# Gradient of two cached-attention blocks on one core: staging tiles, buffer counts, load order and the K transposes are rearranged

## The chip, the core and the metric

The kernel runs on one core of a Trainium2 chip. The time is the device time of one launch in microseconds (us). Of the kernel before there are 11 runs; a comparison of this kernel cannot tell less than about 0.5% from no change.

## What is computed

The forward function has two equal blocks, A and B, with their own inputs; each computes

```
q = x @ wq                         # x [8, 96, 640], wq [640, 32*128]
p = softmax(q k^T / sqrt(128))     # k_cache, v_cache [8, 32, 512, 128]
o = p v
a = o @ wo                         # wo [32*128, 640]
```

and the two results are joined on the last axis. The kernel returns this output and, for a given grad_out [8, 96, 1280], the gradients of all ten inputs (x, k_cache, v_cache, wq and wo of both blocks). Everything is bfloat16. With 8 batch rows b, 32 heads h and two blocks there are 512 pairs (h, b), each with 96 queries and 512 keys.

## The kernel before

One core does block A and then block B. Within a block the heads follow each other, and within a head the eight batch rows. A pair (h, b) passes through stages that are spread over successive **ticks**, one pair entering per tick: transposing K on TensorE (PE) where that is done (`c_s1`, L260), the scores S and their row maximum (`c_s2a`, L271), the exponential E (L284), the normalised P (L304, on GpSimd, POOL), P transposed and the output O from V (`c_s45`, L313), dV (`c_s4`, L341), dP, a row sum and dS (`c_s6`, L371), dS transposed and dQ from K (`c_s78`, L385), dK (`c_s7`, L411). So in each tick PE works on several pairs at once, in different stages.

Per head there is more: wo and wq are loaded (`pA`, L172, from POOL's queue), transposed (`pB`), Q and dO are projected (`pC`, L207: `q_ps`) and transposed (`pD`), O and dQ are transposed back (`qA`), dwo and dwq are made (`qB`, L445; `qD`, L465). Heads are put together in groups of five or six; at the end of a group `gU` (L487) adds the group's part of the output and of dx. With the block's last group the sums go to tiles `ob` and out by DMA.

The order of all this is written by hand: an emitter sorts all steps by a tick and a slot (tables OFF, HK and SLOTS, L45 to L51). A scheduler then takes them in that order, and moves above all DMAs to where their buffers come free; `pinned` (L107) keeps an instruction in program order among those that are pinned.

K and V come from memory in pairs of batch rows, 256 KB a load, from SyncE's queue (SP), into rings of 7 K and 5 V buffers. Of both a transposed copy is needed: V's (`VT`, 3 buffers) is always made by a DMA transpose (`c_xt`, L252, on SP's queue); K's (`KT`, 2 buffers) is made so for the odd pairs of a head, and on PE for the even ones: four 128x128 transposes (L265) per b and a copy out of PSUM on VectorE (DVE, L267). So half of K is transposed on PE.

At the start (`first`), x and grad_out are loaded whole (`setup_nat`, L134) and transposed (`setup_T`, L118). For block B they are needed while block A still runs and still uses its own copies. So they come a second time, in twelve tiles of [128, 640] (160 KB) from POOL's queue (`setup_ld`, L110), into a pool of their own of 6 buffers (`ld_tmp`), and PE transposes them during the last heads of block A. After A is done, the whole arrays follow (L146).

Of the kernel before, what the change touches and what calls it, by code (L numbers as in the profile page):

```python
# [10 lines left out]
F32 = mybir.dt.float32  # L11
# [29 lines left out]
SL_HEAD = 90  # L41
SL_GRP = 95
SL_SETUP = 96

OFF = dict(ldk=-5, ldv=-3, kt=-1, vt=2, s2=3, s3=3, s4=4, s5=5, s6=6, s7=7, s8=8)  # L45
HK = dict(pA=-7, pB=-3, pC0=[-2, 0], pC1=[-1, 0], pD1=1, pD0=2, qA0=13, qA1=17, qB=[20, 17], qD=[(18, 0, 2), (19, 2, 4), (20, 4, 5)])
EV = dict(pB0="act", pB1="dve", pC00="act", pC01="act", pC10="act", pC11="dve", pD0="dve", pD1="dve", qA0="dve", qA1="dve", qB0="act", qB1="act", qD="dve", gU="act")
GSPREAD0 = 9
PRIO_OFF = 2000
# [4 lines left out]
def build_block(tc, em, tick0, blk, x, kc, vc, wq, wo, g_all, out_all, dx, dk, dv, dwq, dwo, ident, ones, pools, HG=6, first=True, groups=None):  # L54
# [47 lines left out]
    HS = pools["HS"]  # L102
    CS = pools["CS"]

    stp = pools["stp"]

    def pinned(ins):  # L107
        return tc.keep_in_program_order(ins)

    def setup_ld(which_, t):  # L110
        def f():
            src_flat = x_flat if which_ == 0 else g_flat
            tmp = stp.tile([128, D], BF16, name="ld_tmp")
            pinned(nc.gpsimd.dma_start(tmp[:], src_flat[t * 128:(t + 1) * 128, :]))
            S[("tmp", which_, t)] = tmp
        return f

# [47 lines left out]
    for i, (which_, t) in enumerate(xg):  # L165
        if not first:
            em.add(tick0 - 12 + i // 2, SL_LOAD, setup_ld(which_, t))
        em.add(tick0 + ((-8 if which_ == 0 else -3) if first else -8 + i // 2), SL_SETUP, setup_T(which_, t))
    em.add(tick0 + (-11 if first else B + OFF["s5"] - 2), SL_LOAD + 1, setup_nat(1))
    em.add(tick0 + (-12 if first else B + OFF["s8"] - 2), SL_LOAD, setup_nat(0))  # L170

    def pA(h):  # L172
        def f():
            wo_h = hst.tile([128, D], BF16, name="wo_h", bufs=HG + 3)
            order = pinned if first and 0 < h < HG + 3 else (lambda ins: ins)
            if h % 2 == 0:
                wq_p = hd.tile([128, DC, 256], BF16, name="wq_p", bufs=2)
                with nc.allow_non_contiguous_dma(reason="wq slice of two heads"):
                    order((nc.sync if first and h == 0 else nc.gpsimd).dma_start(wq_p[:], wq_v[:, :, h * 128:(h + 2) * 128]))
            order(nc.gpsimd.dma_start(wo_h[:], wo[h * 128:(h + 1) * 128, :]))  # L180
            if h % 2 == 1:
                wq_p = HS[(blk, h - 1)]["wq_p"]
            HS[(blk, h)] = dict(wo_h=wo_h, wq_p=wq_p, wq_h=wq_p[:, :, (h % 2) * 128:(h % 2 + 1) * 128])
        return f
# [261 lines left out]
    def qB(h, di):  # L446
        def f():
            st = HS[(blk, h)]
            Onat = st["Onat"]
            if "dwo_sb" not in st:  # L450
                st["dwo_sb"] = hd.tile([128, D], BF16, name="dwo_sb", bufs=1)
                st["dwo_n"] = 0
            dwo_sb = st["dwo_sb"]
            (c0, w) = dsplits[di]
            w_ps = bank([128, w], F32, "dwo_ps")
            for t in range(TT):
                nc.tensor.matmul(w_ps[:], Onat[:, t, :], S["g_nat"][:, t, c0:c0 + w], start=(t == 0), stop=(t == TT - 1))  # L457
# [30 lines left out]
    def gU(g, which, t, gi):  # L488
        def f():
            acc = S.get("out_acc" if which == 0 else "dx_acc")  # L490
            dst_flat = out_flat if which == 0 else dx_flat
            (c0, w) = gsplits[gi]
            o_ps = bank([128, w], F32, "o_ps")
            for hh in range(groups[g]):
                h = GH0[g] + hh
                src = HS[(blk, h)]["OT_h"] if which == 0 else HS[(blk, h)]["dQT_h"]
                rhs = HS[(blk, h)]["wo_h"][:, c0:c0 + w] if which == 0 else HS[(blk, h)]["wqT_h"][:, c0:c0 + w]
                nc.tensor.matmul(o_ps[:], src[:, t * 128:(t + 1) * 128], rhs, start=(hh == 0), stop=(hh == groups[g] - 1))  # L498
            if 0 < g < NG - 1:
                nc.vector.tensor_tensor(acc[:, t, c0:c0 + w], o_ps[:], acc[:, t, c0:c0 + w], op=ALU.add)  # L500
                return
            if g == 0 and NG > 1:
                evac(EV["gU"], acc[:, t, c0:c0 + w], o_ps[:])
                return
            if gi == 0:
                S["ob"] = wk.tile([128, D], BF16, name="ob", bufs=4)
            ob = S["ob"]
            if NG == 1:
                evac(EV["gU"], ob[:, c0:c0 + w], o_ps[:])
            else:  # L510
                nc.vector.tensor_tensor(ob[:, c0:c0 + w], o_ps[:], acc[:, t, c0:c0 + w], op=ALU.add)
            if gi == len(gsplits) - 1:
                (nc.gpsimd if first else nc.sync).dma_start(dst_flat[t * 128:(t + 1) * 128, :], ob[:])
        return f

    NTS = len(tsplits)
    S45 = pools["S45"]
    S78 = pools["S78"]
    for g in range(NG):
        h0 = GH0[g]  # L520
        for hh in range(groups[g]):
            h = h0 + hh
            c0t = tick0 + h * B
            if not (first and h == 0):
                em.add(c0t + HK["pA"], SL_LOAD, pA(h))
            em.add(c0t + HK["pB"], SL_HEAD, pB(h))
            for si in range(NTS):
                em.add(c0t + HK["pC0"][min(si, len(HK["pC0"]) - 1)], SL_HEAD, pC(h, 0, si))
                em.add(c0t + HK["pC1"][min(si, len(HK["pC1"]) - 1)], SL_HEAD, pC(h, 1, si))
            em.add(c0t + HK["pD1"], SL_HEAD, pD(h, 1))  # L530
            em.add(c0t + HK["pD0"], SL_HEAD, pD(h, 0))
            for b in range(B):
                ct = c0t + b
                if b % NB == 0:
                    em.add(tick0 - 12 if first and h == 0 and b == 0 else ct + OFF["ldk"], SLOTS["LOAD"], c_ld(h, b, "K", 7))
                    em.add(ct + OFF["ldv"], SLOTS["LOAD"], c_ld(h, b, "V", 5))
                    if (b // NB) % 2 == 1:
                        em.add(ct + OFF["kt"], SLOTS["LOAD"] + 1, c_xt(h, b, "KT", 2))
                    em.add(ct + OFF["vt"], SLOTS["LOAD"] + 1, c_xt(h, b, "VT", 3))
                if (b // NB) % 2 == 0:  # L540
                    em.add(ct + 2, SLOTS["S1"], c_s1(h, b))
                em.add(ct + OFF["s2"], SLOTS["S2A"], c_s2a(h, b))
                em.add(ct + OFF["s2"], SLOTS["S2B"], c_s2b(h, b))
                em.add(ct + OFF["s3"], SLOTS["S3A"], c_s3a(h, b))
                em.add(ct + OFF["s3"], SLOTS["S3B"], c_s3b(h, b))
                em.add(ct + OFF["s5"], SLOTS["S5B"], c_s5b(h, b))
                if b % 2 == 1:
                    em.add(ct + OFF["s4"] + 1, SLOTS["LOAD"], c_st(h, b, "v"))
# [35 lines left out]
def _kernel_impl(tc, A_x, A_k_cache, A_v_cache, A_wq, A_wo, B_x, B_k_cache, B_v_cache, B_wq, B_wo, grad_out,  # L584
# [13 lines left out]
    with ExitStack() as ctx:  # L598
# [3 lines left out]
        make_identity(nc, ident[:])  # L602
        ones = cst.tile([128, 1], BF16, name="ones")
        nc.vector.memset(ones[:], 1.0)
        pools = dict(
            const=P(name="const", bufs=1),
            ps=P(name="ps", bufs=8, space=PSUM),
# [2 lines left out]
            hd=P(name="hd", bufs=2),  # L610
            hst=P(name="hst", bufs=HG + 2),
            grp=P(name="grp", bufs=1),
            stp=P(name="stp", bufs=6),
        )
        pools["S45"] = {}
        pools["S78"] = {}
        pools["HS"] = {}
# [80 lines left out]
```

## Time and profile before

| what | value |
|---|---|
| median of 11 runs | 1745.0 us (1735.7 to 1760.11) |
| the profiled execution: its time | 1745.14 us |
| its span, first to last instruction | 1743.1 us |
| mean granted clock of TensorE | 0.994 |
| busy: ACT, DVE, POOL | 81%, 77%, 60% |
| DMA | 424.69 MB, mean 244 GB/s |
| HBM read, written | 161.09 MB, 159.12 MB |

The span is 2.0 us shorter than the time of the same execution. A busy PE is not PE at its peak: the profile models the end of a matmul, and matmuls are pipelined. What one costs is read from the distance between starts, in the list of instructions in order of time ("timeline"). The busy share of the DMA engines counts every packet in flight, of all queues, over 16 engines; as packets of several queues overlap, it can be over 1. PEclk is the share of its full clock that TensorE was granted.

### The profile page before, as it was taken

The numbers are of one execution on the slowest core, as the hardware profiler recorded it, in microseconds if no ns is written. First come the engines' busy times: TensorE is split into PE (matmuls) and PEld (weight loads), VectorE is DVE, ScalarE is ACT, GpSimd is POOL, SyncE is SP. The second block draws the span as 40 slices with busy tenths as digits, with TensorE's granted clock in tenths as the row PEclk, the third lists the DMA queues.
The fourth block names the chain that finished last, engine by engine and source line by source line (L and its number), as shares of the span: only waits on it lengthen the run. The fifth ranks groups of instructions, "written<-read, shape, count | busy, mean of one in ns | idle before, by whom it ended". The sixth has DMA issues, their size and how long they took to land.

```text
span 1743.1 us, 57509 instructions
## 1 busy us (share of the span) xinstructions
PE 1678.8 (96%) x21730; PEld 1328.2 (76%) x21944; DVE 1334.1 (77%) x3043; ACT 1414.6 (81%) x4023; POOL 1049.1 (60%) x1759
## 2 busy tenths in 40 slices
PE   7999999999999999999898999999999999999998
PEld 6787777778778778777677777787787787787785
DVE  5887677778878878877676876787788787788785
ACT  6998788878879879878667997897798797798793
POOL 3676566556556656557465665565565665565563
PEclk9999999999999999999999999999999999999999
DMA  9999999999989989999999999999999899999893
GB/s 252 266 287 244 244 246 233 266 221 249 247 229 264 262 218 261 260 223 232 228 273 251 271 264 215 240 273 239 218 261 244 222 276 241 219 277 245 205 256 123
DMA packets 603751, 424.69 MB, mean 244 GB/s; under 512 B 425633, under 2 KB 560417, under 8 KB 603473
## 3 DMA queue, kind: packets, MB, share of 16 engines
q1 hardware_dynamic: 548752, 239.22, 69.2%
q0 software_dynamic: 54720, 181.78, 32.8%
q8 instruction: 172, 2.82, 0.7%
q14 instruction: 107, 0.87, 0.2%
HBM read 161.09 MB, written 159.12 MB: 184 GB/s over the span
## 4 chain that ended last, share of the span: by engine, by line
PE 74%; DVE 9%; ACT 7%; DMA 5%; issue 3%; POOL 1%; SPq 0%; ACTq 0%; DVEq 0%; POOLq 0%
PE o_ps L498 11%; PE q_ps L223 11%; PE dwo_ps L457 5%; PE dwq_ps L477 5%; PE S_ps L278 5%; PE dV_ps L349 5%; PE dK_ps L419 5%; PE dP_ps L377 5%; PE dq_dst_ps L402 4%; PE optp_ps L332 4%; PE optp_ps L325 4%; PE dq_dst_ps L395 3%; DVE negm L280 3%; DVE dS_sb L381 3%; ACT E_sb L290 2%
## 5 line engine op out<-in xcount | busy, mean ns | idle before, releaser
L309 POOL TENSOR_SCALAR P_sb<-E_sb,rinv 96x512 bf16<-96x512 bf16 x512 | 350.8, 685 | 403.2 <-DVE rinv L300 399.8
L290 ACT ACTIVATE E_sb<-S_ps,negm 96x512 bf16<-96x512 f32 x512 | 349.2, 682 | 191.4 <-DVE negm L280 186.3
L381 DVE SCALAR_TENSOR_TENSOR dS_sb<-dP_ps,dl_ps,P_sb 96x512 bf16<-96x512 f32 x512 | 383.0, 748 | 97.5 <-PE dl_ps L379 72.1
L280 DVE TENSOR_REDUCE negm<-S_ps 96x1 f32<-96x512 f32 x512 | 347.5, 679 | 64.1 <-PE S_ps L278 59.4
L422 ACT ACTIVATE dK_sb<-dK_ps 128x512 bf16<-128x512 f32 x512 | 301.3, 589 | 59.4 <-PE dK_ps L419 38.1
L352 ACT ACTIVATE dV_sb<-dV_ps 128x512 bf16<-128x512 f32 x512 | 313.5, 612 | 8.7 <-DMA out_dram<-dV_sb 8.6
L358 POOL DMA_DIRECT2D out_dram<-dV_sb x256 | 194.8, 761 | 130.0 <-ACT dV_sb L352 90.9
L338 ACT ACTIVATE PT_sb<-optp_ps 128x384 bf16<-128x384 bf16 x512 | 254.6, 497 | 1.6 <-PE optp_ps L332 1.6
L358 POOL DMA_DIRECT2D out_dram<-dK_sb x256 | 192.3, 751 | 38.2 <-ACT dK_sb L422 28.5
L367 POOL TENSOR_TENSOR prod<-OT_h,dOT_h 128x96 bf16<-128x96 bf16 x512 | 186.1, 363 | 43.4 <-ACT OT_h L335 35.7
L377 PE MATMUL dP_ps<-VT,dOT_h 128*96 128x512 bf16 x512 | 195.8, 382 | 6.0 <-DMA VT<-V_sb 5.6
L349 PE MATMUL dV_ps<-dOnat_h,P_sb 96*128 96x128 bf16 x2048 | 199.1, 220 | 0.0
L419 PE MATMUL dK_ps<-Qnat_h,dS_sb 96*128 96x128 bf16 x2048 | 197.9, 219 | 0.0
L404 DVE COPY dST_sb<-dq_dst_ps 128x384 bf16<-128x384 bf16 x512 | 176.3, 344 | 22.6 <-PE dq_dst_ps L402 22.6
L402 PE MATMUL dq_dst_ps<-ident,dS_sb 96*128 96x96 bf16 x2048 | 172.3, 206 | 11.8 <-DVE dS_sb L381 11.7
L332 PE MATMUL optp_ps<-ident,P_sb 96*128 96x96 bf16 x2048 | 172.4, 206 | 8.7 <-POOL P_sb L309 8.2
L325 PE MATMUL optp_ps<-PT_sb,V_sb 128*128 128x96 bf16 x2048 | 172.5, 206 | 3.0 <-ACT dV_sb L352 3.0
L395 PE MATMUL dq_dst_ps<-dST_sb,K_sb 128*128 128x96 bf16 x2048 | 170.7, 206 | 0.0
L395 PEld LDWEIGHTS <-K_sb 128*128 128x128 bf16 x2048 | 131.8, 98 | 29.4 <-issue 5.2
L300 DVE RECIPROCAL rinv<-rowsum 96x1 f32<-96x1 f32 x512 | 80.3, 157 | 88.2 <-ACT E_sb L290 78.3
L223 PE MATMUL q_ps<-gT,woT_h 128*128 128x512 bf16 (+1 forms) x625 | 137.0, 325 | 0.9
L457 PE MATMUL dwo_ps<-g_nat,Onat 128*128 128x128 bf16 (+1 forms) x708 | 129.6, 294 | 3.6 <-ACT dK_sb L422 0.2
(84 smaller groups left out, 3789.8 us busy)
## 6 DMA issues: line engine op xcount, KB each, us to landing
out_dram<-dV_sb POOLq DMA_DIRECT2D x256, 256.0 KB, 4.7
out_dram<-dK_sb POOLq DMA_DIRECT2D x256, 256.0 KB, 4.8
K_sb<-in_A_k_cache_dram SPq DMA_DIRECT2D x128, 256.0 KB, 4.7
V_sb<-in_A_v_cache_dram SPq DMA_DIRECT2D x128, 256.0 KB, 4.8
K_sb<-in_B_k_cache_dram SPq DMA_DIRECT2D x128, 256.0 KB, 4.5
V_sb<-in_B_v_cache_dram SPq DMA_DIRECT2D x128, 256.0 KB, 4.6
out_dram<-dwo_sb POOLq DMA_DIRECT2D x64, 160.0 KB, 4.5
out_dram<-dwq_sb POOLq DMA_DIRECT2D x32, 320.0 KB, 4.7
```

Source lines behind the costliest of these rows:

```text
L223: nc.tensor.matmul(q_ps[:], lhs(c), rhsT[:, c, t0:t0 + w], start=(c == 0), stop=(c == DC - 1))
L280: nc.vector.tensor_reduce(negm[:], S_ps[:], axis=AX.X, op=ALU.max, negate=True)
L290: nc.scalar.activation(E_sb[:], st["S_ps"][:], ACT.Exp, bias=st["negm"][:], scale=1.0, accum_out=rowsum[:])
L309: nc.gpsimd.tensor_scalar(P_sb[:], st["E_sb"][:], st["rinv"][:], 0.0, op0=ALU.mult, op1=ALU.add)
L349: nc.tensor.matmul(dV_ps[:, c * 128:(c + 1) * 128], P_sb[:, c * 128:(c + 1) * 128], hs["dOnat_h"][:, b * 128:(b + 1) * 128], start=True, s ...
L352: nc.scalar.activation(SB[(blk, h, b // 2, "v")][:, b % 2], dV_ps[:], ACT.Identity, scale=1.0)
L358: nc.gpsimd.dma_start(dst[b - 1:b + 1, h].rearrange("b (p c) d -> p b (c d)", c=KC), SB.pop((blk, h, b // 2, which))[:])
L377: nc.tensor.matmul(dP_ps[:], hs["dOT_h"][:, tok], st["VT"], start=True, stop=True)
L381: nc.vector.scalar_tensor_tensor(dS_sb[:], dP_ps[:], dl_ps[:, 0:1], st["P_sb"][:], op0=ALU.subtract, op1=ALU.mult)
L395: nc.tensor.matmul(dQT_ps, st["K_sb"][:, c, :], st["dST_sb"][:, c * Sq:(c + 1) * Sq], start=(c == 0), stop=(c == KC - 1))
L419: nc.tensor.matmul(dK_ps[:, c * 128:(c + 1) * 128], dS_sb[:, c * 128:(c + 1) * 128], hs["Qnat_h"][:, b * 128:(b + 1) * 128], start=True, s ...
L422: nc.scalar.activation(SB[(blk, h, b // 2, "k")][:, b % 2], dK_ps[:], ACT.Identity, scale=1.0)
```

## The change

- **Staging.** The pool `ld_tmp` goes. The tiles of x for block B are now taken out of the ring of K buffers, those of grad_out out of the ring of V buffers.
- **Buffers.** K 7 to 9, V 5 to 6, KT 2 to 3, VT 3 to 4; the loads and DMA transposes are placed earlier (OFF: ldk -5 to -9, ldv -3 to -5, kt -1 to -2, vt 2 to 0).
- **K on PE.** `k_on_pe`: the first pair of every head, and the third only in heads of even number. So 3 of 8 pairs are transposed on PE, not 4 of 8; the others go by DMA.
- **Output rows.** The tiles `ob` (4 buffers of their own) become buffers of `dwo_sb`, which has 3 instead of 1.
- **Loads of wo and wq.** All but those of the very first head are pinned in program order (before, those of heads 1 to 8 of block A alone); `pA` is placed a tick later.
- **The start.** The transposes of grad_out, the projection of dO and its transposes are put behind the first projection of Q, so that the first S stands ahead of them.
- **PE warmed.** 32 matmuls of a tile of ones, with a result that nobody reads, are the first that PE does.

```diff
-OFF = dict(ldk=-5, ldv=-3, kt=-1, vt=2, s2=3, ...
-HK = dict(pA=-7, ...
+NK_SB, NV_SB = 9, 6
+OFF = dict(ldk=-9, ldv=-5, kt=-2, vt=0, s2=3, ...
+HK = dict(pA=-6, ...
...
-            tmp = stp.tile([128, D], BF16, name="ld_tmp")
-            pinned(nc.gpsimd.dma_start(tmp[:], src_flat[t * 128:(t + 1) * 128, :]))
+            nm, nb_ = ("K_sb", NK_SB) if which_ == 0 else ("V_sb", NV_SB)
+            tmp = kvp.tile([128, NB, KC, 128], BF16, name=nm, bufs=nb_)[:].rearrange("p a c d -> p (a c d)")[:, 0:D]
+            pinned(nc.gpsimd.dma_start(tmp, src_flat[t * 128:(t + 1) * 128, :]))
...
-        em.add(tick0 + ((-8 if which_ == 0 else -3) if first else -8 + i // 2), SL_SETUP, setup_T(which_, t))
+        em.add(tick0 + ((-8 if which_ == 0 else 3) if first else -8 + i // 2), SL_SETUP, setup_T(which_, t))
...
-            order = pinned if first and 0 < h < HG + 3 else (lambda ins: ins)
+            order = (lambda ins: ins) if first and h == 0 else pinned
...
-                st["dwo_sb"] = hd.tile([128, D], BF16, name="dwo_sb", bufs=1)
+                st["dwo_sb"] = hd.tile([128, D], BF16, name="dwo_sb", bufs=3)
...
-                S["ob"] = wk.tile([128, D], BF16, name="ob", bufs=4)
+                S["ob"] = hd.tile([128, D], BF16, name="dwo_sb", bufs=3)
...
+    def k_on_pe(h, b):
+        return b // NB == 0 or (b // NB == 2 and h % 2 == 0)
...
+            fh = first and h == 0
...
-                em.add(c0t + HK["pC1"][min(si, len(HK["pC1"]) - 1)], SL_HEAD, pC(h, 1, si))
-            em.add(c0t + HK["pD1"], SL_HEAD, pD(h, 1))
-            em.add(c0t + HK["pD0"], SL_HEAD, pD(h, 0))
+                em.add(c0t + (3 if fh else HK["pC1"][min(si, len(HK["pC1"]) - 1)]), SL_HEAD + (7 if fh else 0), pC(h, 1, si))
+            em.add(c0t + (3 if fh else HK["pD1"]), SL_HEAD + (8 if fh else 0), pD(h, 1))
+            em.add(c0t + (4 if fh else HK["pD0"]), SL_HEAD, pD(h, 0))
...
-                    if (b // NB) % 2 == 1:
-                        em.add(ct + OFF["kt"], SLOTS["LOAD"] + 1, c_xt(h, b, "KT", 2))
-                    em.add(ct + OFF["vt"], SLOTS["LOAD"] + 1, c_xt(h, b, "VT", 3))
-                if (b // NB) % 2 == 0:
+                    if not k_on_pe(h, b):
+                        em.add(ct + OFF["kt"], SLOTS["LOAD"] + 1, c_xt(h, b, "KT", 3))
+                    em.add(ct + OFF["vt"], SLOTS["LOAD"] + 1, c_xt(h, b, "VT", 4))
+                if k_on_pe(h, b):
                     em.add(ct + 2, SLOTS["S1"], c_s1(h, b))
...
+        warm = cst.tile([128, 128], BF16, name="warm")
+        nc.vector.memset(warm[:], 1.0)
...
-            stp=P(name="stp", bufs=6),
...
+        warm_ps = pools["ps"].tile([128, 128], F32, name="warm_ps", tag="bank")
+        for _ in range(32):
+            nc.tensor.matmul(warm_ps[:], warm[:], warm[:], start=True, stop=True)
```

More of the change, by code (lines that the diff above doesn't have):

```diff
@@ L43 @@
 SL_SETUP = 96
-OFF = dict(ldk=-5, ldv=-3, kt=-1, vt=2, s2=3, s3=3, s4=4, s5=5, s6=6, s7=7, s8=8)
-HK = dict(pA=-7, pB=-3, pC0=[-2, 0], pC1=[-1, 0], pD1=1, pD0=2, qA0=13, qA1=17, qB=[20, 17], qD=[(18, 0, 2), (19, 2, 4), (20, 4, 5)])
+NK_SB, NV_SB = 9, 6
+OFF = dict(ldk=-9, ldv=-5, kt=-2, vt=0, s2=3, s3=3, s4=4, s5=5, s6=6, s7=7, s8=8)
+HK = dict(pA=-6, pB=-3, pC0=[-2, 0], pC1=[-1, 0], pD1=1, pD0=2, qA0=13, qA1=17, qB=[20, 17], qD=[(18, 0, 2), (19, 2, 4), (20, 4, 5)])
 EV = dict(pB0="act", pB1="dve", pC00="act", pC01="act", pC10="act", pC11="dve", pD0="dve", pD1="dve", qA0="dve", qA1="dve", qB0="act", qB1="act", qD="dve", gU="act")
@@ L103, in build_block @@
     CS = pools["CS"]
-    stp = pools["stp"]
     def pinned(ins):
@@ L534, in build_block @@
                 if b % NB == 0:
-                    em.add(tick0 - 12 if first and h == 0 and b == 0 else ct + OFF["ldk"], SLOTS["LOAD"], c_ld(h, b, "K", 7))
-                    em.add(ct + OFF["ldv"], SLOTS["LOAD"], c_ld(h, b, "V", 5))
-                    if (b // NB) % 2 == 1:
-                        em.add(ct + OFF["kt"], SLOTS["LOAD"] + 1, c_xt(h, b, "KT", 2))
-                    em.add(ct + OFF["vt"], SLOTS["LOAD"] + 1, c_xt(h, b, "VT", 3))
-                if (b // NB) % 2 == 0:
+                    em.add(tick0 - 12 if first and h == 0 and b == 0 else ct + OFF["ldk"], SLOTS["LOAD"], c_ld(h, b, "K", NK_SB))
+                    em.add(ct + OFF["ldv"], SLOTS["LOAD"], c_ld(h, b, "V", NV_SB))
+                    if not k_on_pe(h, b):
+                        em.add(ct + OFF["kt"], SLOTS["LOAD"] + 1, c_xt(h, b, "KT", 3))
+                    em.add(ct + OFF["vt"], SLOTS["LOAD"] + 1, c_xt(h, b, "VT", 4))
+                if k_on_pe(h, b):
                     em.add(ct + 2, SLOTS["S1"], c_s1(h, b))
```

## The prediction

> **What bounds the kernel now.** First I read the page's busy shares and its chain of work that ended last. PE leads, and it is followed back through most of the span.
>
> ```profile
> PE 1678.8 (96%) x21730; PEld 1328.2 (76%) x21944; DVE 1334.1 (77%) x3043; ACT 1414.6 (81%) x4023; POOL 1049.1 (60%) x1759
> PE 74%; DVE 9%; ACT 7%; DMA 5%; issue 3%; POOL 1%; SPq 0%; ACTq 0%; DVEq 0%; POOLq 0%
> ```
>
> Then, by stretches of the span: busy time of PE, PEld, DVE, ACT and POOL with the number of instructions, granted clock, DMA share, GB/s.
>
> ```profile
> 0.00:20.00 20.00, 11.79 (x118) 9.23 (x120) 7.17 (x16) 7.70 (x13) 2.60 (x9) 0.99 0.96 277
> 20.00:50.00 30.00, 26.92 (x335) 21.44 (x336) 21.50 (x51) 26.18 (x74) 18.39 (x32) 0.89 1.02 240
> 100.00:200.00 100.00, 97.47 (x1287) 77.66 (x1295) 74.06 (x167) 87.90 (x252) 64.57 (x108) 1.00 1.14 258
> 800.00:850.00 50.00, 42.72 (x557) 33.58 (x559) 34.85 (x80) 34.78 (x98) 31.70 (x55) 0.97 1.12 215
> 850.00:900.00 50.00, 46.59 (x576) 36.14 (x580) 36.19 (x83) 34.65 (x101) 28.32 (x48) 0.97 1.10 260
> 900.00:1000.00 100.00, 92.43 (x1206) 73.79 (x1214) 74.46 (x172) 80.39 (x231) 64.94 (x109) 0.97 1.10 266
> 1100.00:1700.00 600.00, 589.51 (x7738) 469.60 (x7814) 480.73 (x1100) 499.43 (x1427) 365.56 (x612) 1.00 1.02 244
> ```
>
> In the long stretches PE is busy 97 to 98% at full clock. It falls behind in two places: the first 50 us (11.3 us idle, and a clock of 0.89 over 30 us, worth 3.3 us) and the change of block, 800 to 1000 us (181.7 us busy where 1100 to 1700 would give 196.5, so 14.8 us, and a clock of 0.97 over 200 us, worth 6 us). Both have a cause in PE's list of waits from 800 to 935 us (what waited, for whom: us in total, times, longest):
>
> ```profile
> PE optp_ps L332 <- POOL P_sb L309: 5.8, 2, 5.3
> PE dP_ps L377 <- DMA VT<-V_sb: 5.6, 2, 3.0
> PE optp_ps L325 <- ACT dV_sb L352: 1.4, 1, 1.4
> PE tp_ps L130 <- DMA ld_tmp<-in_grad_out_dram: 0.9, 1, 0.9
> ```
>
> So a gain must come from less work on PE, or from these two places.
>
> **K on PE.** Per two heads, 3 pairs instead of 4 are transposed on PE: 32 pairs or 64 b in the whole kernel lose four transposes and a copy. In PE's list in order of time (start, us) the four take from 809.44 to the next start at 809.66:
>
> ```profile
> 809.44 0.39 PE L265 MATMUL kT_ps<-ident,K_sb 128*128 128x128 bf16 x4
> 809.66 0.33 PE L395 MATMUL dq_dst_ps<-dST_sb,K_sb 128*128 128x96 bf16 x4
> ```
>
> That is 0.22 us, not the four times 219 ns that the groups show, which overlap. 64 x 0.22 = **14.1 us**, all on PE: in the built order they vanish from ticks that also hold projections or other work per head, so PE stays the bound there. DVE loses 64 copies of 412 ns, 26 us, beside PE. What waits on that copy (8.1 us of PEld before S) loses a quarter, and dS, which PE awaits for 11.7 us, comes a little earlier: I take **2 us**, between 0 and 6.
>
> 32 DMA transposes are added, on SP's queue and on the DMA engines. SP issues one in 1.2 to 1.5 us (about 45 us more of its 1743, and it mostly waits). Of the DMA engines' price the page gives a bound: queue q1 spends 69.2% of the span on 548752 packets, 35 ns each, and there are 425633 packets under 512 B to 384 transposes, 1108 each, so 1108 x 35 ns / 16 = 2.4 us of all 16 engines, 78 us for 32. While PE does not wait for K or V this is hidden, and in 1100 to 1700 it does not. The cover is better than before: KT now stands 7 to 11 ticks ahead of its S in the built order (before 7), VT 6 or 7 ahead of its dP (before 4 or 5), a tick being 1743/512 = 3.4 us and a transpose landing in about 5 us. I take 2 us; without cover see the first rival.
>
> **The change of block, what goes.** Both waits for VT stand where a V transposed with 4 or 5 ticks of lead met loads that land late (K_sb at a median of 10.9 us between 800 and 860, 4.7 elsewhere). With two more ticks I expect both gone. With the wait of 0.9 and that of 1.4 behind a POOL that waited for its loads this is at most 7.9 us, and the clock (0.91 in 820 to 840 and 840 to 860, so 3.6 us) with it: 11.5 at most; I take **9**. The 5.3 us for P_sb stand at 916 us, where POOL sits behind DMAs it may not issue yet, just after the whole x of block B and five wo tiles were issued in a row; pinned, those five are spread over later heads. With the clock after it (0.83 in 920 to 940, 3.4 us) it is worth 8.7; x stays, so I take **6**.
>
> **The change of block, what comes.** The staging tiles now wait for K and V buffers, on POOL's queue, in front of P_sb and the stores. In the built order four of the pairs or tiles are issued late, and PE meets their transposes with little work in between. Work by starts in the same list: one tick's fixed part (dq to dl) is 1.38 us, projections 0.21 for 512 columns, transposes 0.055 each. Issue takes 0.56 us, landing 6.1 (median of the x tiles; 4.8 the least of all twelve, 11.4 the median of the grad_out tiles).
>
> - x tile 1: waits for a dQ two ticks ahead; work until it is needed 5.3 us. Wait 0.56 + 6.1 - 5.3 = 1.4.
> - x tiles 2 and 3: wait for the transposes of tiles 0 and 1. Work 1.38 + 20 transposes and 0.2 = 2.7. Wait 4.0.
> - grad_out tiles 2 and 3: the same behind x. Work 1.38 + 0.22 + 12 x 0.107 = 2.9, two issues. Wait 4.3.
> - grad_out tiles 4 and 5: work 5.2. Wait 2.0.
>
> The sum is 11.7 us; with 4.8 it is 6.5, with 11.4 it is 33. The two waits of about 4 would each halve the clock for a while, as 3.0 us did at 834 (1.8 us each): **15.3 us** added. I take 6.1 because only four K and V loads, not eight, are issued beside the tiles in these ticks. K and V themselves are then late, but still 7 ticks ahead.
>
> The Trainium skill prices such a load lower. DMA: Bandwidth & Descriptors (section Anatomy of one DMA) fits 2.0 us plus bytes over 436 GB/s, by which 160 KB would take an estimated 2.4 us. By that the four waits would come to about 0.3 us and the sum below to some 15 us less. The landings of these very tiles in this trace (4.8 to 12.8 us) speak against it, so I use them.
>
> **The start.** Before, the first S starts at 16.84 us, the first dV at 20.13, and P of the second b keeps PE until 22.55. The x transposes end as before, since the second part of x lands at 7.78. Behind them stand 0.8 us of weights' transposes, 1.6 us of Q, its copy 0.6: S at about 12. But the six copies of grad_out on ACT (0.65 each) with E between them then end at about 17, and dO, its transposes and copy follow: first dV at about 19, second P some 2.5 us earlier than before. I take **3 us**. At most it is 9.5 (14.6 lost, less 5.1 until x lands). It can be a loss of up to 3: the first KT is issued behind one more load and a VT, about 1.5 us later than 12.85, and lands 5.1 us later, when S of the third b wants it. The 32 warming matmuls run before 5.08 us (32 x 0.115, the cold pace of the first twenty, is 3.7 us, from about 1.1). They shorten the x transposes, which DVE's copies of 0.49 us bound anyway, so I give them nothing.
>
> **At no price:** output rows in three shared buffers (24 stores, one in about 1.5 ticks, landing in 4.8 us; PE would wait only if DVE were late by ticks), and the pinned loads of wo and wq (a head ahead).
>
> **Sum.** -14.1 - 2 + 2 - 9 - 6 + 15.3 - 3 = -16.8. From the profiled span of 1743.1 this gives 1726.3, and with the 2.0 us around it **1728 us**. The profiled execution took 1745.14, the median is 1745.0, so nothing is to be shifted.
>
> **Rivals.**
>
> - *DMA becomes the bound (slower).* All queues together now use 69.2 + 32.8 + 0.9 = 102.9% of the span, 1794 us; with 78 more 1872. To end in 1726 us the share must hold at 1.083. For it: 1.14 was held from 100 to 200 while PE lost nothing. Against it: 600 us at 1.02, and between 800 and 860, where 1.9 MB of tiles came on top at a share of 1.1, landings doubled. If 1.06, between 1.02 and 1.10, is the most that lasts, the span is 1872/1.06 = 1766 and the time 1768. It decides from a ceiling of 1.08 down.
> - *Staging costs its upper price.* Tiles land in 11.4 us as grad_out's did: 33 + 4 x 1.8 = 40 instead of 15, so 1753. For it: rows of grad_out are strided. Against it: fewer loads beside.
> - *The waits nearly vanish.* Staging at 6.5 without a clock loss, and the start gains its 9.5: 1728 - 8.8 - 6.5 = 1713.
> - *PE's work was not on the path.* If S, E and P's round trip, not PE, sets the tick, taking 0.22 us from PE gives nothing: 1742. The 97 to 98% of PE speaks against it; that the profile models ends speaks a little for it.
>
> **Chances.** Forecast 0.54, waits vanish 0.15, staging dear 0.13, DMA bound 0.10, not on the path 0.08. Faster by over 0.5% (under 1736; about what can be told from no change) is 0.54 + 0.15 = 0.69, within it 0.13 + 0.08 = 0.21, slower 0.10. The range runs from the vanishing waits with some of the start's bound, 1708, to just under the dear staging, 1750.
>
> **What would show it.** K transposes on PE 768, not 1024, at the same 0.22 us per four, and PE still 97 to 98% busy from 1100 on: the 14 us. No PE wait for VT; new PE waits at the transposes of K_sb and V_sb around 800 to 830 us, about 12 us in all. No wait of 5 us for P_sb after that. First S at about 12 us. It is wrong if VT or KT make PE wait in the long stretches, if the DMA share there stays at 1.02 with landings over 7 us, or if the tiles wait far from 12 us.

## The result

The change made the kernel slower: 1781.0 us (median of 12 runs, 1762.63 to 1796.76) against 1745.0 us (1731.15 to 1760.11 in 47 runs), a ratio of 1.0175 with a 95% interval of 1.0144 to 1.0207. The forecast was 1728 us and the range ended at 1750. The profiled execution of the changed kernel is its quickest, 1762.63 us with a span of 1760.6. A ratio leaves out executions over 1.5% above a kernel's quickest, so a kernel with a wide spread looks better by it than by its median; both are given below.

Part of the loss is the clock. TensorE's mean granted clock, as a median over the runs, is 0.987 after and 0.995 before: 1781 x 0.013 = 23 us against 1745 x 0.005 = 9 us. So by this estimate some 14 of the 36 us are time lost to a lower clock, and not waits themselves.

The page of the changed kernel, the lines that answer to those of before, and the queue that carries the transposes:

```profile
PE 1679.6 (95%) x21509; PEld 1323.0 (75%) x21720; DVE 1312.1 (75%) x2980; ACT 1411.8 (80%) x4023; POOL 1053.9 (60%) x1759
...
q1 hardware_dynamic: 582544, 247.62, 72.7%
...
PE 60%; ACT 13%; DMA 11%; DVE 9%; issue 5%; POOL 2%; ACTq 0%; SPq 0%; POOLq 0%; DVEq 0%
```

PE's share of the chain falls from 74 to 60%, and what it loses goes mostly to ACT (7 to 13) and DMA (5 to 11). PE is still 95% busy: a share of busy time does not show that the end is now set elsewhere. The chain alone does not give the size of a loss either: in the run e13 below, at 1752.5 us, it reads much the same (62% PE, 12% ACT, 11% DMA). (The trace of this execution lacks some matmul records, as that of before does, so PE's counts are not compared.)

By stretches, with the columns of before:

```profile
0.00:20.00 20.00, 14.33 (x141) 11.67 (x144) 5.69 (x15) 7.83 (x13) 2.61 (x9) 0.91 1.01 269
20.00:50.00 30.00, 24.91 (x332) 20.25 (x331) 21.53 (x49) 24.88 (x69) 17.42 (x29) 0.92 1.12 273
100.00:200.00 100.00, 95.47 (x1235) 76.17 (x1244) 71.31 (x162) 84.76 (x243) 61.45 (x103) 0.98 1.12 257
800.00:850.00 50.00, 44.58 (x596) 36.51 (x598) 37.97 (x87) 36.33 (x106) 35.08 (x60) 0.97 1.05 263
850.00:900.00 50.00, 48.77 (x625) 38.16 (x630) 38.24 (x89) 38.05 (x110) 31.41 (x53) 1.00 1.06 273
900.00:1000.00 100.00, 87.36 (x1067) 67.83 (x1076) 66.22 (x153) 73.69 (x209) 58.56 (x98) 0.93 1.11 233
1100.00:1700.00 600.00, 581.01 (x7519) 458.17 (x7593) 463.11 (x1055) 491.18 (x1404) 365.51 (x609) 1.00 1.09 246
```

From 1100 to 1700 the DMA share is 1.09 instead of 1.02, and PE is busy 581.0 us instead of 589.5 with less work per pair. From 100 to 200, where the share was high before too (1.14), PE now falls from 97.5 to 95.5 us, with a clock of 0.98. In the first 50 us PE is busy 39.2 us instead of 38.7, of which the 32 warming matmuls are 3.6. Of the block change, 800 to 900 is better than before, 900 to 1000 worse.

A clearer measure of progress is the start of the n-th exponential on ACT (one for each of the 512 pairs), after minus before, in us:

| n | 1 | 16 | 64 | 216 | 240 | 264 | 288 | 384 | 512 |
|---|---|---|---|---|---|---|---|---|---|
| after - before | -3.3 | +2.4 | +5.7 | +3.3 | +6.0 | +0.1 | +5.4 | +12.3 | +16.6 |

The start wins 3 us and has lost them by the 16th pair; the block change (240 to 288) comes out even; the last 224 pairs lose 11 us, where 6 were to be won. This is the quickest execution of the changed kernel, 18 us under the median, so its trace shows only a part of the loss.

PE's waits at the change of block, 800 to 935 us (us in total, times, longest):

```profile
PE dl_ps L379 <- DVE dwo_sb L511: 3.7, 2, 3.2
PE tp_ps L130 <- DMA K_sb<-in_B_x_dram: 2.3, 1, 2.3
PE tp_ps L130 <- DMA V_sb<-in_grad_out_dram: 2.1, 1, 2.1
PE q_ps L223 <- DVE dwo_sb L511: 1.3, 2, 0.6
```

And what is new outside it: ACT's waits for its own stores, which were 8.6 and 3.7 us, and the stores' time to landing (last column), which was 4.7 and 4.8:

```profile
ACT dV_sb L352 <- DMA out_dram<-dV_sb: 19.1, 14, 3.5
ACT dK_sb L422 <- DMA out_dram<-dK_sb: 17.4, 16, 2.8
...
out_dram<-dV_sb POOLq DMA_DIRECT2D x256, 256.0 KB, 5.2
out_dram<-dK_sb POOLq DMA_DIRECT2D x256, 256.0 KB, 5.5
```

ACT copies dV and dK out of PSUM, the memory into which PE writes its results, into two tiles each. When a store lands late, ACT is held, the part of PSUM is not freed, and PE waits for ACT (for `dV_sb` 6.4 us before dP, for `dK_sb` 5.8 before the transposes of wq). No wait for KT or VT appears in PE's list at all.

### The profile page after: what moved, and what is told of

Same layout as the page of the kernel before. It is cut to its first block, busy times and chain, and to the rows that moved or that the text cites. A ratio compares the mean times of both kernels' runs of the same rounds, so it can differ in the third digit from the quotient of the medians.

```text
span 1760.6 us, 57010 instructions
## 1 busy us (share of the span) xinstructions
PE 1679.6 (95%) x21509; PEld 1323.0 (75%) x21720; DVE 1312.1 (75%) x2980; ACT 1411.8 (80%) x4023; POOL 1053.9 (60%) x1759
## 3 DMA queue, kind: packets, MB, share of 16 engines
q1 hardware_dynamic: 582544, 247.62, 72.7%
## 4 chain that ended last, share of the span: by engine, by line
PE 60%; ACT 13%; DMA 11%; DVE 9%; issue 5%; POOL 2%; ACTq 0%; SPq 0%; POOLq 0%; DVEq 0%
PE o_ps L498 11%; PE q_ps L223 8%; DMA out_dram<-dK_sb 5%; PE dwq_ps L477 4%; PE dwo_ps L457 4%; PE S_ps L278 4%; ACT E_sb L290 4%; PE dK_ps L419 4%; DMA out_dram<-dV_sb 4%; PE dV_ps L349 4%; PE dP_ps L377 4%; PE dq_dst_ps L402 3%; PE optp_ps L332 3%; PE optp_ps L325 3%; PE dq_dst_ps L395 3%
## 5 line engine op out<-in xcount | busy, mean ns | idle before, releaser
L290 ACT ACTIVATE E_sb<-S_ps,negm 96x512 bf16<-96x512 f32 x512 | 355.1, 694 | 178.1 <-DVE negm L280 176.2
L422 ACT ACTIVATE dK_sb<-dK_ps 128x512 bf16<-128x512 f32 x512 | 308.3, 602 | 85.3 <-PE dK_ps L419 53.4
L352 ACT ACTIVATE dV_sb<-dV_ps 128x512 bf16<-128x512 f32 x512 | 319.4, 624 | 22.4 <-DMA out_dram<-dV_sb 19.1
L338 ACT ACTIVATE PT_sb<-optp_ps 128x384 bf16<-128x384 bf16 x512 | 261.0, 510 | 1.1 <-PE optp_ps L332 1.1
L402 PE MATMUL dq_dst_ps<-ident,dS_sb 96*128 96x96 bf16 x2048 | 173.4, 207 | 11.8 <-DVE dS_sb L381 11.7
L223 PE MATMUL q_ps<-gT,woT_h 128*128 128x256 bf16 (+1 forms) x624 | 136.9, 325 | 3.6 <-ACT gT L157 1.8
L408 ACT ACTIVATE dQT_h<-dq_dst_ps 128x96 bf16<-128x96 f32 x512 | 132.1, 258 | 4.7 <-DVE dST_sb L404 3.8
```

Of the source, the lines that this page charges most:

```text
L223: nc.tensor.matmul(q_ps[:], lhs(c), rhsT[:, c, t0:t0 + w], start=(c == 0), stop=(c == DC - 1))
L290: nc.scalar.activation(E_sb[:], st["S_ps"][:], ACT.Exp, bias=st["negm"][:], scale=1.0, accum_out=rowsum[:])
L352: nc.scalar.activation(SB[(blk, h, b // 2, "v")][:, b % 2], dV_ps[:], ACT.Identity, scale=1.0)
L422: nc.scalar.activation(SB[(blk, h, b // 2, "k")][:, b % 2], dK_ps[:], ACT.Identity, scale=1.0)
```

## The experiments

First theory, **COUNT**: the 32 added DMA transposes load the DMA engines, stores land later, and PE waits by way of ACT. Rivals: **DEPTH** (the deeper rings crowd the stores) and **REST** (staging, pinned loads, shared output buffers).

### One part undone, or done alone

**e1**, half of K on PE again, the rest as changed:

```
     def k_on_pe(h, b):
-        return b // NB == 0 or (b // NB == 2 and h % 2 == 0)
+        return (b // NB) % 2 == 0
```

> The changed kernel with half of K on TensorE again (32 DMA transposes fewer, 64 four-transposes of 0.22 us more on PE); rings, staging and start stay as changed. Theory COUNT (the 32 added DMA transposes load the DMA engines, the stores of dV and dK land later, ACT is held on its two store buffers, and PE with it): the loss goes, about 1745 us less what the start gives, 1735 to 1750, and ACT's waits for stores fall from 36 us to about 12. Theory DEPTH (deeper K, V, KT, VT rings and earlier loads crowd the stores): it stays slow and pays 11 to 14 us more PE work, about 1790. Theory REST (staging, pinned loads, output rows in dwo_sb): also about 1790.

Measured: 1746.9 us, ratio 1.0014 (0.9978 to 1.0050). The whole loss is gone; with half of K on PE, start, staging, rings, output rows and pinned loads together are worth nothing either way.

**e2**, the kernel before with 3/8 of K on PE alone (the same function put into it):

> The kernel before with 3/8 of K on TensorE and nothing else changed. COUNT: slower, about 1765 to 1780. DEPTH and REST: the PE work saved shows, about 1731 to 1735, since the rings are as before.

Measured: 1798.6 us, 1.0300 (1.0242 to 1.0357), slower than COUNT had it. Here PE does wait for KT, as a stretch of three pairs goes through two KT buffers:

```profile
PE S_ps L278 <- DMA KT<-K_sb: 41.4, 12, 8.2
```

**e3**, the changed kernel with the rings and placements of before:

```
-NK_SB, NV_SB = 9, 6
-OFF = dict(ldk=-9, ldv=-5, kt=-2, vt=0, ...
+NK_SB, NV_SB = 7, 5
+OFF = dict(ldk=-5, ldv=-3, kt=-1, vt=2, ...
...
-                        em.add(ct + OFF["kt"], SLOTS["LOAD"] + 1, c_xt(h, b, "KT", 3))
-                    em.add(ct + OFF["vt"], SLOTS["LOAD"] + 1, c_xt(h, b, "VT", 4))
+                        em.add(ct + OFF["kt"], SLOTS["LOAD"] + 1, c_xt(h, b, "KT", 2))
+                    em.add(ct + OFF["vt"], SLOTS["LOAD"] + 1, c_xt(h, b, "VT", 3))
```

> The changed kernel with the ring sizes and the load placement of the kernel before (K 7, V 5, KT 2, VT 3). COUNT: still slow, 1770 to 1785, since the 32 added transposes stay. DEPTH: about 1731 to 1745. REST: about 1775 to 1780.

Measured: 1810.9 us, 1.0398 (1.0351 to 1.0444), slower than all theories had it. With 3/8 on PE the deeper rings as a whole help; DEPTH, as it was put, falls.

**e4**, wo and wq pinned as before only:

> The changed kernel with the loads of wo and wq pinned only as they were before (heads 1 to 8 of block A). COUNT and DEPTH: no change from the changed kernel, 1775 to 1785. REST, if the pinned loads are its part: 1735 to 1760.

Measured: 1770.0 us, 1.0150 (1.0103 to 1.0197). That lies between the two ranges. The median is 11 us under that of the changed kernel, but the intervals overlap; the pinned loads are at most a part of the loss.

### What a transpose costs

**e5**, the 32 added pairs not transposed at all:

```
+    def c_asis(h, b, name, bufs):
+        def f():
+            for i in range(NB):
+                CS[(blk, h, b + i)][name] = CS[(blk, h, b + i)]["K_sb"].rearrange("p c d -> p (c d)")
+        return f
...
-                    if not k_on_pe(h, b):
+                    if b // NB == 2 and h % 2 == 1:
+                        em.add(ct + OFF["kt"], SLOTS["LOAD"] + 1, c_asis(h, b, "KT", 3))
+                    elif not k_on_pe(h, b):
                         em.add(ct + OFF["kt"], SLOTS["LOAD"] + 1, c_xt(h, b, "KT", 3))
```

> The changed kernel, but the third pair of every odd head (32 pairs) is not transposed at all: its scores are taken from K as it lies, so its outputs are not the reference's. TensorE saves the same 14 us as in the changed kernel, and the 32 added DMA transposes are gone. COUNT: about 1747 - 14 = 1733 (1728 to 1738), the gain that was forecast for the change. If the loss came instead from KT buffers or from the missing work on TensorE (S earlier, other work late), it stays above 1760.

Measured: 1743.6 us, 0.9981 (0.9950 to 1.0012). The loss is gone, so it takes the 32 transposes to have it, as COUNT says. But the gain of 14 us is not there either, and COUNT's range of 1728 to 1738 is missed: against e1, which differs only in the 64 b of PE work and their copies on DVE, the ratios give -0.0033 +- 0.0048, that is 6 us less, between 14 less and 3 more; the medians give 3.3.

**e6**, a plain copy of the same 256 KB in the place of those transposes (from the tile of K to a KT buffer, in SyncE's queue):

```
+    def c_copy(h, b, name, bufs):
...
+            nc.sync.dma_start(XT[:], <K tile>[:].rearrange("p a c d -> p (a c) d"))
...
+                    if b // NB == 2 and h % 2 == 1:
+                        em.add(ct + OFF["kt"], SLOTS["LOAD"] + 1, c_copy(h, b, "KT", 3))
```

> As the run before, but the 32 pairs are moved to KT by a plain copy DMA of the same 256 KB, in the place of the DMA transpose (outputs not the reference's). If bytes, the issue on SP's queue or the KT buffers are the price of a transpose: about 1775 to 1785, as the changed kernel. If it is the many small packets of the transpose: 1733 to 1745.

Measured: 1805.3 us, 1.0323 (1.0259 to 1.0387): dearer than the transposes, and above both ranges. Queue q1 has 144 packets for each copy and 1056 for each transpose, and takes 1.5 against 2.2 us of all 16 engines (72.7% of 1760.6, or 70.1% of 1797.3, less e5's 69.7% of 1736.6, over 32). So fewer packets and less engine time did not make it cheaper. Neither the small packets nor the transpose as such is needed for the loss.

That left two readings of COUNT. **LOAD**: the price of a transpose is the time of the DMA engines. **ORDER**: it is the KT buffers and what SyncE's queue holds up.

**e11**, e5 with 32 transposes of three quarters of the size, into a tile that nobody reads:

```
+            junk = kvp.tile([128, 6, 128], BF16, name="junk", bufs=1)
+            nc.sync.dma_start_transpose(junk[:], <K tile>[:, 0:768])
```

> The run without transposes of the third pair of odd heads (1743.6 us; outputs not the reference's), to which 32 DMA transposes of 6 of the 8 blocks of those K tiles are added on SP's queue, into a tile that nobody reads. Nobody waits for them and no KT buffer is taken. LOAD: the cost is that of the DMA engines' time, 0.75 x 37 us = 28 us, so 1765 to 1775. ORDER (the cost comes from KT buffers, and from what SP's queue holds up behind a transpose that waits for one): 1744 to 1752.

Measured: 1752.6 us, 1.0017 (0.9981 to 1.0053), 9 us over e5 by medians, 6 +- 8 by ratios. By LOAD 28 were expected; ORDER's range ended at 1752. Most of the loss therefore comes with KT's buffers or with the order in which SyncE issues, not with the load.

**e8** and **e9**: half of K on PE with output buffers of their own (e8), and the same with 32 fewer V transposes (e9):

```
-                st["dwo_sb"] = hd.tile(..., name="dwo_sb", bufs=3)
+                st["dwo_sb"] = hd.tile(..., name="dwo_sb", bufs=1)
-                S["ob"] = hd.tile(..., name="dwo_sb", bufs=3)
+                S["ob"] = wk.tile(..., name="ob", bufs=3)
```

> Half of K on TensorE again as in the first run, and the output rows have three buffers of their own again, dwo_sb one. If the waits behind dwo_sb (4.5 us of TensorE for o_ps, and the clock after it) are a cost of the shared buffers: 1738 to 1742. If they come from the DMA engines' load alone: 1747, no change.

> Half of K on TensorE and own output buffers, as in the run at 0.9992 of the kernel before; besides, V of the third pair of odd heads (32 pairs) is not transposed, dP is taken from V as it lies (outputs not the reference's). TensorE's work is the same, the DMA engines lose 32 transposes. If the DMA engines bound the kernel before as well as TensorE (theory LOAD): 1715 to 1730. If TensorE alone bounds it and DMA only matters once 32 are added: 1742 to 1747, no change.

Measured: e8 1745.7 us, 0.9992 (0.9966 to 1.0017); e9 1737.3 us, 0.9950 (0.9917 to 0.9984). With the same work on PE, 32 transposes fewer are worth 8 us by medians, 7 +- 7 by ratios. That lies between the two ranges. It suggests that the transposes hold up the kernel with half of K on PE too, if less than LOAD had it. The interval only just leaves out zero, and the run does not separate the engines' time from SyncE's queue and the VT buffers.

**e10**, 5/8 of K on PE, own output buffers:

> The changed kernel with 5/8 of K on TensorE (pairs 0 and 2, and pair 3 of even heads) and own output buffers: 32 DMA transposes fewer than before, 14 us more on TensorE. If TensorE alone bounds the kernel with half: about 1760. If the DMA engines bind as much (LOAD), part of the 14 us comes back: 1745 to 1752. Under 1740 would be a better kernel than both.

Measured: 1742.6 us, 0.9977 (0.9955 to 0.9999). 14 us more work on PE and 32 transposes fewer cost nothing (-3 +- 6 us against e8). Its page:

```profile
PE 1702.7 (98%) x22232; PEld 1343.4 (77%) x22232; DVE 1355.7 (78%) x3108; ACT 1418.1 (81%) x4023; POOL 1052.8 (60%) x1759
...
PE 77%; DVE 9%; ACT 7%; DMA 3%; issue 2%; POOL 1%; ACTq 0%; SPq 0%; DVEq 0%; POOLq 0%
```

It has the lowest median of the study among the versions that compute the same outputs, but 0.23% is less than the measurement can tell from no change.

### What the rings do

SyncE's list showed the next clue: where one transpose stands directly behind another. Start and duration of each issue in the changed kernel (us):

```profile
1180.69 2.04 SPq L246 DMA_DIRECT2D K_sb<-in_B_k_cache_dram  x1
1182.82 6.85 SPq L255 DMA_TRANSPOSE VT<-V_sb  x1
1189.77 3.17 SPq L255 DMA_TRANSPOSE KT<-K_sb  x1
1193.03 0.54 SPq L246 DMA_DIRECT2D V_sb<-in_B_v_cache_dram  x1
1193.66 0.42 SPq L246 DMA_DIRECT2D K_sb<-in_B_k_cache_dram  x1
1194.17 2.50 SPq L255 DMA_TRANSPOSE VT<-V_sb  x1
1196.77 1.49 SPq L255 DMA_TRANSPOSE KT<-K_sb  x1
```

The same place in e13 (below):

```profile
1182.66 1.02 SPq L246 DMA_DIRECT2D K_sb<-in_B_k_cache_dram  x1
1183.73 2.35 SPq L255 DMA_TRANSPOSE VT<-V_sb  x1
1191.66 1.23 SPq L255 DMA_TRANSPOSE KT<-K_sb  x1
1192.99 0.55 SPq L246 DMA_DIRECT2D V_sb<-in_B_v_cache_dram  x1
1193.63 0.42 SPq L246 DMA_DIRECT2D K_sb<-in_B_k_cache_dram  x1
1194.14 1.42 SPq L255 DMA_TRANSPOSE VT<-V_sb  x1
```

In both programs KT follows VT in the queue. In e13 KT still has to wait for its own K to land, and 5.6 us lie between the two issues. In the changed kernel K has landed already, KT starts within 0.1 us, and the issue itself is held: in the whole trace 104 of 416 transposes start within 0.3 us of the end of another's issue and take 3.0 us, the others 1.85; before, it is 2 of 384, and the mean issue is 1.5 us. The VT ahead of KT stands behind a load, and its issue is the longest here, 6.85 us, so a place behind another transpose is not the only thing that goes with a long issue. The DMA share is 1.10 and 1.32 while these two issues last, against 1.09 from 1100 to 1700. Whether the issues crowd the engines or full engines hold the issues is open. Theory **BUNCH**: this is what the nine K buffers do with three KT buffers.

**e13**, seven K buffers and their loads 5 ticks ahead, the rest as changed:

```
-NK_SB, NV_SB = 9, 6
-OFF = dict(ldk=-9, ...
+NK_SB, NV_SB = 7, 6
+OFF = dict(ldk=-5, ...
```

> The changed kernel with 7 K buffers, loaded 5 ticks ahead, instead of 9 and 9 ticks. Theory BUNCH (K lies ready, so SyncE issues KT's transpose directly behind VT's, both are held, and the burst delays loads and stores): KT waits for its own K load again, under 20 transposes stand directly behind another, and the time is 1750 to 1765. If the K ring has no part in it: 1775 to 1790 and about 100 of them.

Measured: 1752.5 us, 1.0042 (1.0004 to 1.0081), and 10 directly behind another. Two K buffers *fewer* take back 28 us by medians (23 +- 9 by ratios).

**e17**, nine K buffers, the loads placed 5 ticks ahead:

> The changed kernel with its 9 K buffers, but the K loads placed 5 ticks ahead instead of 9. If the place of the loads makes K lie ready: KT waits for its K load again, few transposes directly behind another, 1750 to 1760. If it is the number of buffers: 1775 to 1785, some 100 directly behind another.

Measured: 1785.4 us, 1.0213 (1.0160 to 1.0267), 102 directly behind another. So it is the number of buffers, not the place in the tables. In code e17 and e13 differ in that number alone: 33 us by medians, 30 +- 12 by ratios. This execution is nearer to its kernel's median than the profiled one of the changed kernel, and shows the path better (ACT's waits):

```profile
ACT dK_sb L422 <- DMA out_dram<-dK_sb: 29.6, 16, 5.3
ACT dV_sb L352 <- DMA out_dram<-dV_sb: 15.3, 11, 3.9
```

That is 45 us of ACT held by stores, against 12 before, 26 in e13 and 12 in e5. The stores of dV and dK land in 5.4 and 5.7 us here, in 4.8 and 5.2 in e13.

**e12**, the kernel before with 3/8 of K on PE and a third KT buffer (`ob` 3, `ld_tmp` 5 for the room):

> The kernel before with 3/8 of K on TensorE (1798.6 us in the run above) and three KT buffers instead of two; for their room three output buffers instead of four and five staging tiles instead of six. If the 41 us of TensorE's waits for KT come from the two buffers when three pairs in a row go by DMA: 1770 to 1780, about the changed kernel. If from the loads' depth or the DMA engines: 1790 to 1800.

Measured: 1758.2 us, 0.9981 (0.9933 to 1.0030; 1732.74 to 1771.08), against e2's 1798.6, and better than either range. One KT buffer is worth 40 us by medians. The median is 13 us over that of before; the ratio shows no loss.

**e14** and **e15**: the changed kernel with all rings and placements of before but three KT buffers; with four KT buffers and eight K.

> The changed kernel with all rings and placements of the kernel before (K 7, V 5, VT 3) but three KT buffers; staging, start, output rows and pinned loads as changed. If the deeper rings are what costs: 1750 to 1765, as the kernel before with 3/8 and three KT buffers (1758.2). If staging, output rows or pinned loads cost when the DMA engines are full: 1775 to 1785.

> The changed kernel with four KT buffers instead of three, K 8 instead of 9 for their room. If SyncE's waits for KT buffers (153 us for S) are what bunches and delays the transposes: 1750 to 1765. BUNCH by a K that lies ready: no gain, 1775 to 1790.

Measured: e14 1775.6 us, 1.0145 (1.0071 to 1.0219); e15 1766.3 us, 1.0101 (1.0068 to 1.0135). Both have few transposes directly behind another (6 and 10) and are slower than before all the same; e15 takes back 15 us of the loss by medians, e14 5. In e14 PE waits 10.5 us for VT, which has a buffer fewer than in e13, and 6.9 us at once behind dwo_sb; in e15 it waits 13.5 us for the staging tiles of x, which come out of a K ring with a buffer fewer:

```profile
PE tp_ps L130 <- DMA K_sb<-in_B_x_dram: 13.5, 5, 4.5
```

But the profiled execution of e15 took 1753.8 us, 12 less than its median, so these waits do not explain the median. e14 fell into the range of its second reading, and pairs of runs on record agree with that. e14 has the rings and placements of e12, but staging, start, output rows and pinned loads as changed, and is 17 us slower by medians (29 +- 15 by ratios). e3 and e2, both with two KT buffers, differ in the same way by 12 us (17 +- 13). So REST (with the start) is not free where five of eight K pairs go by DMA and the rings are as before, though it was free with half of K on PE (e1). Which of its parts costs was not taken apart there.

So BUNCH is at most a part. The lists of e14 and e15 suggest that with this DMA load a ring that is a buffer short shows up as waits.

**e7**, three store buffers for dV and for dK in the changed kernel, K 8 and V 5 for their room:

> The changed kernel with three instead of two buffers for dV_sb and dK_sb; for their room K has 8 and V 5 buffers. COUNT by way of the stores (ACT held on its store buffers): ACT's waits for stores go to under 8 us of 36, and the time falls to 1755 to 1765. If the store wait only stands where another wait would (K, V, KT or VT come late instead, since the DMA engines have no more to give): 1775 to 1790.

Measured: 1779.6 us, 1.0162 (1.0095 to 1.0229). ACT's waits for stores are gone, and others stand in their place in PE's list:

```profile
PE dP_ps L377 <- DMA VT<-V_sb: 14.3, 11, 2.5
PE tp_ps L130 <- DMA K_sb<-in_B_x_dram: 13.9, 4, 4.3
...
PE S_ps L278 <- DMA KT<-K_sb: 7.2, 7, 2.1
PE tp_ps L130 <- DMA V_sb<-in_grad_out_dram: 7.1, 3, 3.0
```

So more store buffers did not bring the time back, and the lateness showed elsewhere. As K and V gave up a buffer each, the run does not settle what the store buffers alone are worth. (61 transposes stand directly behind another here, with eight K buffers.)

**e16** and **e18**: own output buffers in the changed kernel; e13 with own output buffers and three store buffers.

> The changed kernel with three output buffers of their own and one dwo_sb. If the shared buffers are a part of the loss: TensorE's waits behind dwo_sb (8.3 us) and the clock after them go, 1768 to 1773. If not: 1778 to 1785.

> The changed kernel with 7 K buffers loaded 5 ticks ahead (1752.5 us), own output buffers, and in the room that this leaves three buffers each for dV_sb and dK_sb. If ACT's waits for its stores (26 us there, passed on to TensorE) are what is left of the price of the 32 transposes: 1738 to 1746, at the kernel before or a little under. If the DMA engines' load shows elsewhere (VT, KT, staging tiles): 1748 to 1756, no change.

Measured: e16 1777.9 us, 1.0128 (1.0045 to 1.0212), not to be told from the changed kernel; e18 1748.0 us, 0.9966 (0.9931 to 1.0002; 1724.24 to 1772.41). e18 has no store waits, but PE waits 15.4 us for KT and 8.6 once behind `ob`. It is no better than before by its median (1748.0 against 1744.9). Against e13 it is 4.5 us quicker by medians, 13 +- 9 by ratios.

The kernels with 3/8 of K on PE, by what KT waits for:

| kernel | K, KT buffers | KT's waits for its own K load, us | transposes directly behind another | median, us |
|---|---|---|---|---|
| e12, e13, e14, e18 | 7, 3 | 453, 391, 405, 410 | 2, 10, 6, 7 | 1758, 1753, 1776, 1748 |
| e15 | 8, 4 | 401 | 10 | 1766 |
| e7 | 8, 3 | 259 | 61 | 1780 |
| after, e4, e16, e17 | 9, 3 | 85, 92, 89, 90 | 104, 107, 106, 102 | 1781, 1770, 1778, 1785 |
| e2, e3 | 7, 2 | 157, 128 | 74, 74 | 1799, 1811 |

Where the KT buffer comes free last (nine K on three KT, seven on two), the issue is bunched; where the K load lands last, it is spread by itself. All the bunched ones take 1770 us or more, but so does e14, which is not bunched. That nine K buffers instead of seven cost some 30 us in this kernel is shown (e13 and e17). That they do so by way of the held issue, and that this delays the stores, is argued from the times and the landings, and not shown by itself: no run spread the same issues by other means.

## Why the prediction was wrong, by its steps

- **"So a gain must come from less work on PE."** Only in part. 14 us off PE gave 3 to 6 us where no transpose was added (e5 against e1; 14 is just within the interval), and 14 us onto PE cost nothing where 32 transposes were taken away (e10). PE busy for 97 to 98% looked like one bound; the DMA transposes were a second one close behind it, as far as e9 and e10 tell. The price of the four transposes on PE itself was right. PE's list, start and us:

```profile
701.31 0.38 PE L265 MATMUL kT_ps<-ident,K_sb 128*128 128x128 bf16 x4
701.53 0.33 PE L395 MATMUL dq_dst_ps<-dST_sb,K_sb 128*128 128x96 bf16 x4
```

- **The 2 us for waits on dS and KT_pe.** Next to nothing: dq_dst_ps waits 11.7 us for dS as before, and PEld's wait for KT_pe goes from 8.1 to 7.3 us.
- **"The cover is better than before ... I take 2 us" for 32 DMA transposes.** This is the step that failed. The price on the DMA engines was right (2.2 us of all 16 each, 2.4 was the bound), and so was the cover: no wait for KT or VT. The lead time in ticks was the wrong cover. What it did not cover were the *other* transfers beside them, stores above all (e17's list), and SyncE's queue. Measured, where 2 us were taken: +9 us with seven K buffers (e13 against e5, which has nine; 11 +- 9 by ratios), and 28 more with nine (23 +- 9), where I had counted the deeper ring as pure cover.
- **The change of block.** The VT waits and the 5.3 us for P_sb went, as said. The tiles wait 2.3 + 2.1 = 4.4 us instead of 11.7: the size was off, as they land in 4.8 and 5.1 us instead of the 6.1 taken. From the 240th to the 288th exponential the change comes out at -0.6 us; -9 - 6 + 15.3 was +0.3. The total is right by luck, since its terms were not: the tiles wait less than taken, and the next step was wrong.
- **"At no price: output rows in three shared buffers."** PE waits 8.3 us behind `dwo_sb` in the span, DVE 9.4 us for stores of it, and the clock is 0.90 and 0.85 in 900 to 920 and 920 to 940. With own buffers and half of K on PE (e8) the same 48 pairs gain 12 us on before, where e1 gains 1. By the median of whole runs it is small (e8 against e1 1 us, e16 against the changed kernel 3 us, both within their intervals).
- **The start.** First S at 13.2 us (12 said), first dV at 21.0 (19 said; 20.1 before), and nothing of the 3 us is kept by the 16th pair.
- **The first rival** had the right engine, at a chance of 0.10. Its time, 1768, is near the profiled 1762.6 by way of a share of 105.8% for all queues, its 1.06. But a fixed ceiling is not the mechanism: e13 holds 106.9% and e12 107.2% in less time.
- **The tests named in advance.** "Wrong if VT or KT make PE wait" and "landings over 7 us" did not fire. They looked at the loads that the change makes, and at none of the transfers beside them. The third, "if the tiles wait far from 12 us", did: 4.4 us, in the direction of a gain. PE from 1100 on is 96.8% busy, just under the 97 to 98% forecast.
- **Two slips in the working**, neither of which changes the forecast. With a landing of 2.4 us the terms as written give 0.26 + 0.62 = 0.9 us of waits, not 0.3. The share that a span of 1726 us needs is 1872/1726 = 1.085; 1.083 goes with 1728, the time.

So, in medians: before 1745, staging, start and the rest at half +2 (e1), PE's work -3 (e5), 32 transposes +9 (e13), nine K buffers on three KT +28: 1781. By ratios the steps are +2, -6, +11 and +23. Each step but the last is near or within its interval; the last is what the runs show clearly. Open stay what REST costs in the changed kernel itself, where its staging was not tried alone, why e14 is 23 us slower than e13 beyond the VT and dwo_sb waits named, and how nine K buffers delay the stores.

## What to carry to other kernels

When one engine is 97% busy, look for the second bound before you move work to it: take some of *its* work away without giving the first engine more (e9), or give the first engine more (e10), and see whether the time follows. A transfer that nobody waits for can still delay the stores and loads beside it, so its price is looked for in waits on tiles that the change never touches. A deeper ring is not only cover: here two K buffers more cost some 30 us, and one KT buffer more gained 40. So rings that feed each other are sized together. A likely way, not shown by itself, is that a load that comes earlier lets two costly transfers be issued together which its late landing had kept apart.

## What the runs showed of the hardware

Where SyncE often issues a DMA transpose directly behind another, the issue takes longer: 3.0 us against 1.85 in the changed kernel, 3.0 to 3.4 against 1.7 to 2.0 in the six others with over 60 such cases that put no copies between. Where it is rare it need not: the ten in e13 took 1.5 us on average, the two in the kernel before 1.4. A plain copy from tile to tile in its place made the kernel no quicker (e6, 1805 us), though it took 1.5 instead of 2.2 us of the engines. The Trainium skill, Advanced Engine Details and Errata, section X-Bar Transpose (TRN2), says that transposes are as fast as plain DMAs, with 350 to 400 GB/s expected. The kernel's time does not speak against the first half (e6), but the engine time does, 2.2 against 1.5 us. 256 KB in 2.2 us are 119 GB/s; that is an estimate from packet times beside loads and stores, where packets overlap.

TensorE's clock can fall after shorter waits than I had taken. One wait of 2.3 us, for the x tile at 820.7 to 823.0, is followed by a stretch at half clock (PE busy, then the other engines; clock third from the end):

```profile
820.00:823.50 3.50, 1.23 (x15) 0.91 (x14) 0.96 (x4) 1.13 (x3) 1.40 (x3) 1.00 1.15 282
824.00:827.00 3.00, 3.00 (x32) 2.78 (x30) 1.60 (x6) 2.31 (x7) 1.45 (x3) 0.50 0.79 264
828.00:831.00 3.00, 2.93 (x50) 2.54 (x48) 2.24 (x7) 1.49 (x6) 2.23 (x4) 1.00 0.80 202
```

32 matmuls in 3 us at half clock, 50 at full. Before the end of the span the half clock lasts 3.4 or 6.8 us each time in the traces of before and after (10.2 once each in six of the experiments), so by estimate it costs a busy PE 1.7 or 3.4 us more than the wait. It does not follow every such wait: the 2.1 us for the grad_out tile at 836 us, and 2.5 and 2.4 us for the same kinds of tile in e5, had none behind them. Waits of this size may be why e3 and e6 have low clocks (medians of 0.979 and 0.982); no run tested that.
